# A block-diagonal product in two matmuls of 288 columns, and its result copied out of PSUM by ScalarE before the norm

## The chip, the cores and the metric

The kernel runs on one core of a Trainium2 chip. The metric is the device time of one execution in microseconds; the kernel before has a median of 944.4 us in 3 runs (943.82 to 945.24). The profile shown is of one execution of 944.21 us, whose instructions span 942.4 us, at a mean granted TensorE clock of 0.999.

A core has engines that run beside each other: TensorE (in the profile PE for its matmuls and PEld for its weight loads), VectorE (DVE), ScalarE (ACT), GpSimd (POOL) and SyncE (SP), which here issues the transfers. TensorE writes its results to PSUM, a memory of eight banks of 512 fp32 columns over 128 partitions; VectorE and ScalarE read them there and write to the large memory, SBUF.

## The reference

A linear attention with a norm, whose result is the input of a gated pair of matrix products:

```python
# q, k, v: (8, 8, 576, 64), g_norm: (64,)
kv  = einsum('bhsd,bhse->bhde', k, v)            # 64 x 64 for each head
out = einsum('bhsd,bhde->bhse', q, kv)
rms = sqrt(mean(out * out, axis=-1, keepdims=True) + 1e-6)
x   = out / rms * g_norm                         # then (B, H, S, D) -> (B*S, H*D) = 4608 x 512
# w_in: (512, 2048), w_out: (2048, 512), float64
h  = x @ w_in
sp = max(h, 0) + log1p(exp(-abs(h)))             # softplus
y  = (h * erf(sp)) @ w_out                       # 4608 x 512
```

## The kernel before

Two heads are handled at once, as the two diagonal 64x64 blocks of a 128x128 matrix. There are 8 batch entries (T = 0 to 7) with 4 pairs of heads each (p = 0 to 3): 32 attention steps. Of the 576 rows of a pair, 512 are the main part (G = 512) and 64 the tail (R = 64); the tails of all entries are gathered in `x_last` and go through norm and products as a ninth group (T = 8). The attention steps of group T+1 are dealt out as small pieces between the large products of group T, whose matmuls are at line 462 (`n_ps`, `m_ps`) and, for the first two groups, at lines 520 and 692.

The pieces of one step, with the lines of the profile at the side. `halves` is true for T = 2 to 7, so for 24 of the 32 steps. `bank(...)` gives one of two PSUM tiles of one bank each (`ps_at`).

```python
def products():
    kv_ps = st["kv"] = bank("kv_ps")
    for c in range(C):                           # L297: k^T v, both heads
        for i in range(2):
            nc.tensor.matmul(kv_ps[s, s], lhsT=ks[rows, i, c], rhs=vs[rows, i, c], ...)
    if p % 2 == 0:                               # L305: the tails of two pairs, transposed
        nc.tensor.transpose(kv_ps[:, q_tail], q_last[:, p // 2], ident)
    ...
    for i in range(2):                           # L312: the blocks into bd
        nc.vector.tensor_copy(out=bd[s, s], in_=kv_ps[s, s])
    if p % 2 == 0:                               # L315
        nc.vector.tensor_copy(out=tails[T], in_=kv_ps[:, q_tail])
    st["tail"] = tails[T][:, p % 2 * R : p % 2 * R + R]
    qt_ps = bank("qt_ps")
    for j in range(J):                           # L319: q transposed
        nc.tensor.transpose(qt_ps[:, j * P : j * P + P], qs[:, j], ident)
    nc.scalar.copy(st["qT"], qt_ps)              # L320

def apply():
    qT, o_ps, kv_ps = st["qT"], bank("se_ps"), st.pop("kv")
    nc.tensor.matmul(kv_ps[:, o_tail], lhsT=bd, rhs=st.pop("tail"), ...)   # L324: 64 columns
    nc.tensor.matmul(o_ps, lhsT=bd, rhs=qT, ...)                           # L325: 512 columns
    nc.vector.tensor_copy(out=x_last[:, p, T * R : T * R + R], in_=kv_ps[:, o_tail])
    st["o"] = o_ps
    nc.scalar.activation(qT, o_ps, AF.Square)    # L328

def halve():                                     # the squares as a sum of two fp32r tiles
    nc.vector.tensor_copy(out=hi, in_=sq)        # L338
    nc.vector.tensor_tensor(out=lo, in0=sq, in1=hi.bitcast(FP32), op=ALU.subtract)

def mean(table=True):
    ms = st["ms"] = bank("ms_ps")
    if halves:                                   # L346, L347
        nc.tensor.matmul(ms, lhsT=mean_w, rhs=st.pop("hi"), start=True, stop=False)
        nc.tensor.matmul(ms, lhsT=mean_w, rhs=st.pop("lo"), start=False, stop=True)
    ...
    nc.scalar.activation(r, ms, AF.Ln, bias=eps_col)      # L358
    nc.scalar.activation(r, r, AF.Exp, scale=-0.5)        # L359
    nc.scalar.activation(u, r, AF.Square)                 # L360

def norm():                                      # L366, L369, L378
    nc.vector.scalar_tensor_tensor(out=u, in0=ms, scalar=EPS, in1=u, ...)
    nc.vector.scalar_tensor_tensor(out=u, in0=u, scalar=3.0, in1=r, ...)
    nc.vector.scalar_tensor_tensor(out=x, in0=st.pop("o"), scalar=gm_col, in1=u, ...)

def split():                                     # L405, L408, L411
    thirds(st.pop("x"), *(form[:, p] for form in x_forms[T]))
```

`x_forms` are the three fp32r forms of the normed `x` (a high part, a low part and a scaled sum) that the products at line 462 take. Each of those products is eight matmuls into `n_ps` (high and low part) and four into `m_ps` (the sum), each of 512 columns.

Of the kernel before, what the change touches and what calls it, by code (L numbers as in the profile page):

```python
# [39 lines left out]
FP32 = mybir.dt.float32  # L40
# [3 lines left out]
AF = mybir.ActivationFunctionType  # L44
ALU = mybir.AluOpType
PSUM = bass.MemoryType.PSUM
# [8 lines left out]
FIRST = 2  # L55
# [5 lines left out]
def kernel(  # L61
# [10 lines left out]
    nc = tc.nc  # L72
    P = 128
    B, H, S, D = q.shape
    DM, DF = moe_w_in.shape[0], moe_w_in.shape[1] // 2
    J = 4
    G = J * P
    R = S - G
# [8 lines left out]
    attp = ctx.enter_context(tc.tile_pool(name="attp", bufs=1))  # L87
# [5 lines left out]
    first_w = room.enter_context(tc.tile_pool(name="first_w", bufs=1, side="right"))  # L93
    gate = room.enter_context(tc.tile_pool(name="gate", bufs=7, side="right"))
    early = early_room.enter_context(tc.tile_pool(name="early", bufs=2))
    ps_at = ctx.enter_context(tc.tile_pool(name="ps_at", bufs=2, space=PSUM))
    ps_h = ctx.enter_context(tc.tile_pool(name="ps_h", bufs=2, space=PSUM))
    ps_o = ctx.enter_context(tc.tile_pool(name="ps_o", bufs=1, space=PSUM))

    ctx.enter_context(tc.manual_schedule())  # L100

# [51 lines left out]
    for i in range(2):  # L153
        nc.gpsimd.dma_start(
            out=g_col[i * D : i * D + D, :], in_=g_norm.rearrange("(d one) -> d one", one=1)
# [11 lines left out]
    ident = const.tile([P, P], FP32, name="ident")  # L167
    make_identity(nc, ident)
    mean_w = const.tile([P, P], FP32R, name="mean_w")
# [13 lines left out]
    x_last = const.tile([P, KC, G], FP32, name="x_last")  # L183
# [79 lines left out]
    xT, x_forms, tails = {}, {}, {}  # L263
# [5 lines left out]
    def attention(T, p, pools=None):  # L269

        st = {}

        halves = FIRST <= T < B
        bd = bd_kv[:, (T * NP + p) % 2, :]

        q_tail, o_tail = slice(P, 2 * P), slice(2 * P, 2 * P + R)

        def bank(name):
            pool, tag = (pools or {}).get(name, (ps_at, "at"))
            return pool.tile([P, G], FP32, name=name, tag=tag)  # L280

        def square_tile(name):

            if T == 0:
                return gate.tile([P, G], FP32, name=name, tag="h")
            return attp.tile([P, G], FP32, name=name, tag="qT")

        def products():

            kv_ps = st["kv"] = bank("kv_ps")  # L290
            ks, vs, qs = (x.pop((T, p)) for x in (k_sb, v_sb, q_sb))
            C = chunks(T)
            for c in range(C):
                rows = slice(0, S // C + (c < S % C))
                for i in range(2):
                    s = slice(i * D, i * D + D)
                    nc.tensor.matmul(  # L297
                        kv_ps[s, s],
                        lhsT=ks[rows, i, c],
                        rhs=vs[rows, i, c],  # L300
                        start=(c == 0),
                        stop=(c == C - 1),
                    )
            if p % 2 == 0:
                nc.tensor.transpose(kv_ps[:, q_tail], q_last[:, p // 2], ident)  # L305
            if p == NP - 2:
                for i in range(NP):
                    load_last(T + 1, i)
            st["qT"] = square_tile("qT")
            for i in range(2):  # L310
                s = slice(i * D, i * D + D)
                nc.vector.tensor_copy(out=bd[s, s], in_=kv_ps[s, s])  # L312
            if p % 2 == 0:
                tails[T] = attp.tile([P, P], FP32, name="qT_last", tag="t")
                nc.vector.tensor_copy(out=tails[T], in_=kv_ps[:, q_tail])  # L315
            st["tail"] = tails[T][:, p % 2 * R : p % 2 * R + R]
            qt_ps = bank("qt_ps")
            for j in range(J):
                nc.tensor.transpose(qt_ps[:, j * P : j * P + P], qs[:, j], ident)  # L319
            nc.scalar.copy(st["qT"], qt_ps)  # L320

        def apply():
            qT, o_ps, kv_ps = st["qT"], bank("se_ps"), st.pop("kv")
            nc.tensor.matmul(kv_ps[:, o_tail], lhsT=bd, rhs=st.pop("tail"), start=True, stop=True)  # L324
            nc.tensor.matmul(o_ps, lhsT=bd, rhs=qT, start=True, stop=True)  # L325
# [4 lines that stand above are left out]
        def square():  # L330
            st["o"], st["qT"] = x_last[:, p, :], square_tile("sq")
            nc.scalar.activation(st["qT"], st["o"], AF.Square)

        def halve():
            sq = st.pop("qT")
            hi = st["hi"] = attp.tile([P, G], FP32R, name="sq_hi", tag="rms_r")
            lo = st["lo"] = attp.tile([P, G], FP32R, name="sq_lo", tag="sq_lo")
            nc.vector.tensor_copy(out=hi, in_=sq)  # L338
            nc.vector.tensor_tensor(out=lo, in0=sq, in1=hi.bitcast(FP32), op=ALU.subtract)

        def mean(table=True):
            ms = st["ms"] = bank("ms_ps")
            if halves:


                nc.tensor.matmul(ms, lhsT=mean_w, rhs=st.pop("hi"), start=True, stop=False)  # L346
                nc.tensor.matmul(ms, lhsT=mean_w, rhs=st.pop("lo"), start=False, stop=True)  # L347
                u = square_tile("u")
            else:
                u = st.pop("qT")  # L350
                nc.tensor.matmul(ms, lhsT=mean_w.bitcast(FP32), rhs=u, start=True, stop=True)  # L351
            if T > 0:
                r = attp.tile([P, G], FP32, name="rms_r", tag="rms_r")
                exp_ln_table()
            else:
                r = gate.tile([P, G], FP32, name="rms_r", tag="s")
            st["u"], st["r"] = u, r
            nc.scalar.activation(r, ms, AF.Ln, bias=eps_col)  # L358
            nc.scalar.activation(r, r, AF.Exp, scale=-0.5)  # L359
            nc.scalar.activation(u, r, AF.Square)  # L360
            if table and (T > 0 or p == NP - 1):
                softplus_table()

        def norm():
            ms, u, r = (st.pop(name) for name in ("ms", "u", "r"))
            nc.vector.scalar_tensor_tensor(  # L366
                out=u, in0=ms, scalar=EPS, in1=u, op0=ALU.add, op1=ALU.mult
            )
            nc.vector.scalar_tensor_tensor(  # L369
                out=u, in0=u, scalar=3.0, in1=r, op0=ALU.subtract, op1=ALU.mult  # L370
            )
            if T < FIRST:
                if T not in xT:
                    xT[T] = wide.tile([P, KC, G], FP32, name="xT", tag="ab"[T])
                x = xT[T][:, p, :]
            else:
                x = st["x"] = x_new.tile([P, G], FP32, name="x", tag="x")
            nc.vector.scalar_tensor_tensor(  # L378
                out=x,
                in0=st.pop("o"),  # L380
                scalar=gm_col,
                in1=u,
                op0=ALU.mult,
                op1=ALU.mult,
            )

        def split():
            if T >= FIRST:
                thirds(st.pop("x"), *(form[:, p] for form in x_forms[T]))

        def loads():
            load_pair(T * NP + p + 2)

        if T == 0:
            return products, apply, halve, mean, norm
        if T == B:
            return lambda: None, square, lambda: None, mean, norm, split

        pieces = ((products,), (apply,), (halve, loads)) if halves else ((products, loads), (apply,), ())
        return (*(partial(chain, *group) for group in pieces), mean, norm, split)  # L400


# [111 lines left out]
    o_ps = {}  # L514
# [129 lines left out]
    for n in range(FIRST * FC + 1):  # L644
        T, f = divmod(n, FC)
        if n == FC:
            early_room.close()
            late = ctx.enter_context(tc.tile_pool(name="late", bufs=1))
            x_new = ctx.enter_context(tc.tile_pool(name="x_new", bufs=1))
            acc = ctx.enter_context(tc.tile_pool(name="acc", bufs=1))  # L650
            w_in_p = ctx.enter_context(tc.tile_pool(name="w_in_p", bufs=BATCH))
            low = low_room.enter_context(tc.tile_pool(name="low", bufs=1))
            forms = late.tile([P, 3, KC, G], FP32R, name="x_forms0")
            x_forms[FIRST] = [forms[:, i] for i in range(3)]
# [25 lines left out]
        elif T < FIRST:  # L680
# [10 lines left out]
            for i, c in blocks:  # L691
                nc.tensor.matmul(  # L692
                    plain[i],
                    lhsT=w_in_sb[:, c, i % FC * P : i % FC * P + P],
                    rhs=xT[T][:, c, :],
                    start=(c == 0),
                    stop=(c == KC - 1),
# [89 lines left out]
    for m in range(first_batch, batches + 1):  # L787
        T, b = divmod(m, NB)
# [127 lines left out]
```

## Time and profile before

| | |
|---|---|
| median of 3 runs | 944.4 us (943.82 to 945.24) |
| span of the profiled execution | 942.4 us |
| product and result of one attention step among the large products, from 500.94 to 525.67 us | 24.73 us |
| in it: TensorE, VectorE, ScalarE busy | 24.73, 19.94, 15.91 us |
| the copy of `qt_ps` (L320), the square of `se_ps` (L328) | 584, 580 ns |
| Ln, Exp, Square of the mean (L358, L359, L360) | 688, 632, 633 ns |
| norm (L366, L369, L378) | 684, 691, 751 ns |
| one table load on ScalarE | 1283 ns |

The profile names a group of instructions by its line, its engine and what it writes and reads (out<-in). A mean duration of a matmul's record is not its cost: the records overlap, and their ends are modelled. What one costs is the distance between its start and that of the next.

The timeline gives start and duration of each run of equal instructions, in us from the span's start; what stands in brackets is the idle time of the engine before it, and what ended it.

### The profile page before, as it was taken

The numbers are of one execution on the slowest core, as the hardware profiler recorded it, in microseconds if no ns is written. First come the engines' busy times: TensorE is split into PE (matmuls) and PEld (weight loads), VectorE is DVE, ScalarE is ACT, GpSimd is POOL, SyncE is SP. The second block draws the span as 40 slices with busy tenths as digits, with TensorE's granted clock in tenths as the row PEclk, the third lists the DMA queues.
The fourth block names the chain that finished last, engine by engine and source line by source line (L and its number), as shares of the span: only waits on it lengthen the run. The fifth ranks groups of instructions, "written<-read, shape, count | busy, mean of one in ns | idle before, by whom it ended". The sixth has DMA issues, their size and how long they took to land.

```text
span 942.4 us, 11743 instructions
## 1 busy us (share of the span) xinstructions
PE 924.8 (98%) x4272; PEld 683.4 (73%) x4272; DVE 742.6 (79%) x1056; ACT 615.6 (65%) x825; POOL 2.4 (0%) x10
## 2 busy tenths in 40 slices
PE   6999999999999999999999999999999999999997
PEld 4444445666688888888888888888888888888886
DVE  3999858887577787877778888878887877787667
ACT  3899776776766666666666666666666666665551
POOL 1000000000000000000000000000000000000000
PEclk9999999999999999999999999999999999999999
DMA  9766406899699998998899889998896778778871
GB/s 257 276 204 207 150 1 227 318 351 335 214 363 335 309 325 283 306 311 307 280 287 314 294 298 309 311 303 296 293 325 260 263 253 345 284 286 287 353 263 46
DMA packets 111842, 259.78 MB, mean 276 GB/s; under 512 B 43864, under 2 KB 69544, under 8 KB 111784
## 3 DMA queue, kind: packets, MB, share of 16 engines
q1 hardware_dynamic: 110152, 256.73, 78.7%
q10 hardware_dynamic: 1568, 2.29, 0.8%
q8 instruction: 34, 0.56, 0.2%
q14 instruction: 24, 0.20, 0.1%
q0 software_dynamic: 64, 0.00, 0.0%
HBM read 224.40 MB, written 34.60 MB: 275 GB/s over the span
## 4 chain that ended last, share of the span: by engine, by line
PE 92%; DVE 4%; DMA 2%; ACT 1%; issue 0%; SPq 0%; DVEq 0%
PE n_ps L462 45%; PE m_ps L462 22%; PE o_ps L520 10%; PE h_ps L692 6%; PE se_ps L325 3%; PE kv_ps L297 2%; PE qt_ps L319 2%; DMA w_raw<-in_moe_w_in_dram 1%; PE ms_ps L351 1%; DMA v_sb<-in_v_dram 1%; DVE h L876 1%; DVE e L445 1%; PE ms_ps L346 1%; PE ms_ps L347 1%; PE kv_ps L324 1%; DVE e L440 0%
## 5 line engine op out<-in xcount | busy, mean ns | idle before, releaser
L462 PE MATMUL n_ps<-x_forms,w_in_parts 128*128 128x512 f32 x896 | 232.5, 401 | 0.1
L462 PE MATMUL n_ps<-w_out_parts,g_forms 128*128 128x512 f32 x928 | 231.2, 391 | 0.0
L462 PEld LDWEIGHTS n_ps<-w_out_parts,g_forms 128*128 128x128 f32 x928 | 174.2, 188 | 38.4 <-issue 1.4
L462 PEld LDWEIGHTS n_ps<-x_forms,w_in_parts 128*128 128x128 f32 x896 | 166.8, 188 | 43.1 <-issue 9.3
L852 ACT ACTIVATE s<-h 128x512 f32<-128x512 f32 x112 | 71.0, 633 | 178.9 <-DVE h L445 178.9
L445 DVE TENSOR_TENSOR h<-m_ps,h 128x512 f32<-128x512 f32 x116 | 79.7, 687 | 59.8 <-ACT h L837 43.8
L462 PE MATMUL m_ps<-w_out_parts,g_forms 128*128 128x512 f32 x464 | 124.2, 389 | 0.0
L462 PE MATMUL m_ps<-x_forms,w_in_parts 128*128 128x512 f32 x448 | 120.0, 390 | 0.0
L520 PE MATMUL o_ps<-w_out_sb,h_sb 128*128 128x512 f32 x224 | 100.8, 593 | 0.3 <-DVE h_sb L642 0.3
L462 PEld LDWEIGHTS m_ps<-w_out_parts,g_forms 128*128 128x128 f32 x464 | 87.1, 188 | 18.0
L462 PEld LDWEIGHTS m_ps<-x_forms,w_in_parts 128*128 128x128 f32 x448 | 84.1, 188 | 17.7
L445 DVE TENSOR_TENSOR e<-m_ps,e 128x512 f32<-128x512 f32 x116 | 80.2, 692 | 18.2 <-PE m_ps L462 10.9
L440 DVE SCALAR_TENSOR_TENSOR e<-n_ps,e 128x512 f32<-128x512 f32 x88 | 60.3, 685 | 39.2 <-PE n_ps L462 39.2
L520 PEld LDWEIGHTS o_ps<-w_out_sb,h_sb 128*128 128x128 f32 x224 | 42.3, 190 | 48.9 <-issue 46.6
L411 DVE SCALAR_TENSOR_TENSOR g_forms<-g_forms 128x1024 fp32r<-128x1024 f32 x58 | 71.1, 1225 | 2.0
L408 DVE TENSOR_TENSOR g_forms<-h,g_forms 128x1024 fp32r<-128x1024 f32 x58 | 70.6, 1217 | 1.7 <-ACT g_forms L405 1.4
L876 DVE TENSOR_TENSOR h<-h,s 128x1024 f32<-128x1024 f32 x58 | 68.3, 1218 | 0.7 <-ACT s L856 0.7
L837 ACT ACTIVATE h<-n_ps 128x512 f32<-128x512 f32 x112 | 65.5, 585 | 3.4 <-PE n_ps L462 3.4
L405 ACT ACTIVATE g_forms<-h 128x1024 fp32r<-128x1024 f32 x58 | 58.9, 1059 | 12.2 <-PE m_ps L462 8.7
L692 PE MATMUL h_ps<-xT,w_in_sb 128*128 128x512 f32 x144 | 64.9, 594 | 0.7 <-DVE w_in_sb L240 0.6
L106 ACT ACT_TABLE_LOAD x44 | 56.5, 1283 | 0.8
L856 ACT ACTIVATE s<-s 128x1024 f32<-128x1024 f32 x56 | 56.2, 1052 | 0.3
(98 smaller groups left out, 1013.3 us busy)
## 6 DMA issues: line engine op xcount, KB each, us to landing
w_out_parts<-w_out SPq DMA_DIRECT2D x116, 768.0 KB
w_in_parts<-w_in SPq DMA_DIRECT2D x112, 768.0 KB
w_in<-w_new SPq DMA_DIRECT2D x16, 768.0 KB
q_sb<-in_q_dram SPq DMA_DIRECT2D x32, 256.0 KB
w_raw<-in_moe_w_out_dram SPq DMA_DIRECT2D x8, 1024.0 KB
out_dram<-e SPq DMA_DIRECT2D x32, 256.0 KB
k_sb<-in_k_dram SPq DMA_DIRECT2D x28, 287.5 KB
v_sb<-in_v_dram SPq DMA_DIRECT2D x28, 287.5 KB
```

The lines of the kernel that those rows point to most:

```text
L106: nc.scalar.preload_act_table_set("softplus")
L405: nc.scalar.activation(high, x, AF.Copy, scale=1.0 + 2.0**-13)
L408: nc.vector.tensor_tensor(out=low, in0=x, in1=high.bitcast(FP32), op=ALU.subtract)
L411: nc.vector.scalar_tensor_tensor(out=both, in0=low.bitcast(FP32), scalar=SHIFT, in1=high.bitcast(FP32), op0=ALU.mult, op1=ALU.add,)
L440: nc.vector.scalar_tensor_tensor(out=out_, in0=ps, scalar=scale, in1=out_, op0=ALU.mult, op1=ALU.add)
L445: nc.vector.tensor_tensor(out=out_, in0=ps, in1=out_, op=ALU.add)
L462: nc.tensor.matmul(ps, lhsT=weights(form, k), rhs=moving(form, k), start=(form == forms[0] and k == 0), stop=(form == forms[-1] and k == 3),)
L520: nc.tensor.matmul(o_ps[j], lhsT=g[:, j * P : j * P + P], rhs=w_out_sb[:, f, :], start=(f == 0), stop=last,)
L692: nc.tensor.matmul(plain[i], lhsT=w_in_sb[:, c, i % FC * P : i % FC * P + P], rhs=xT[T][:, c, :], start=(c == 0), stop=(c == KC - 1),)
L837: nc.scalar.activation(h[:, i], n_ps, AF.Copy, scale=SHIFT - 1.0)
L852: nc.scalar.activation(s[:, i], h[:, i], AF.Softplus)
L876: nc.vector.tensor_tensor(out=part(h, half), in0=part(h, half), in1=part(s, half), op=ALU.mult)
```

## The change

For the 24 steps with `halves`, one PSUM tile of two banks takes the place of the two tiles of one bank. Each bank holds one half of the work: first kv and the tail in one and the transposed q in the other, then, in each, 256 columns of the main result and 32 of the tail, and at last 256 columns of the mean beside the result. So the product with the block-diagonal matrix is two matmuls of 288 columns, where it was one of 512 and one of 64, and the mean is two times two matmuls of 256 columns. The transposed q and the tail are therefore laid side by side in SBUF, in two rows of 288. To give the one tile back early, ScalarE copies the result (into `x`) and the mean (into `ms_sb`) to SBUF, and the norm reads them there. The other steps keep the two tiles of one bank, whose pool is closed when the second group begins.

The diff, cut to its core:

```diff
         def bank(name):
+            if T >= FIRST:
+                return two_banks()[:, name in ("qt_ps", "se_ps")]
             pool, tag = (pools or {}).get(name, (ps_at, "at"))
             return pool.tile([P, G], FP32, name=name, tag=tag)
+        def two_banks():
+            if "two" not in st:
+                st["two"] = ps_two.tile([P, 2, G], FP32, name="at_ps", tag="at")
+            return st["two"]
+        HG, HR = G // 2, R // 2
...
         def products():
...
+            if halves:
+                tail = tails.pop(T) if p % 2 else kv_ps[:, P : P + R]
+                nc.vector.tensor_copy(out=st["qT"][:, :, HG:], in_=twofold(tail))
+                if p % 2 == 0:
+                    tails[T] = attp.tile([P, R], FP32, name="qT_next", tag="t")
+                    nc.vector.tensor_copy(out=tails[T], in_=kv_ps[:, P + R : 2 * P])
...
+            if halves:
+                nc.scalar.copy(st["qT"][:, :, :HG], twofold(qt_ps))
...
         def apply():
+            if halves:
+                qT, two = st.pop("qT"), two_banks()
+                for i in range(2):
+                    nc.tensor.matmul(
+                        two[:, i, : HG + HR], lhsT=bd, rhs=qT[:, i], start=True, stop=True
+                    )
+                nc.vector.tensor_copy(
+                    out=twofold(x_last[:, p, T * R : T * R + R]), in_=two[:, :, HG : HG + HR]
+                )
+                o_ps = two[:, :, :HG]
+                qT = st["qT"] = qT[:, :, :HG]
+                nc.scalar.activation(qT, o_ps, AF.Square)
+                x = st["x"] = x_new.tile([P, G], FP32, name="x", tag="x")
+                st["o"] = twofold(x)
+                nc.scalar.copy(st["o"], o_ps)
+                return
...
         def mean(table=True):
-            ms = st["ms"] = bank("ms_ps")
+            ms = st["ms"] = two_banks()[:, :, HG:] if halves else bank("ms_ps")
             if halves:
-                nc.tensor.matmul(ms, lhsT=mean_w, rhs=st.pop("hi"), start=True, stop=False)
-                nc.tensor.matmul(ms, lhsT=mean_w, rhs=st.pop("lo"), start=False, stop=True)
+                hi, lo = (twofold(st.pop(name)) for name in ("hi", "lo"))
+                for i in range(2):
+                    nc.tensor.matmul(ms[:, i], lhsT=mean_w, rhs=hi[:, i], start=True, stop=False)
+                    nc.tensor.matmul(ms[:, i], lhsT=mean_w, rhs=lo[:, i], start=False, stop=True)
...
             nc.scalar.activation(r, ms, AF.Ln, bias=eps_col)
+            if halves:
+                st["ms"] = twofold(attp.tile([P, G], FP32, name="ms_sb", tag="sq_lo"))
+                nc.scalar.copy(st["ms"], ms)
             nc.scalar.activation(r, r, AF.Exp, scale=-0.5)
...
         if n == FC:
             early_room.close()
+            at_room.close()
+            ps_two = ctx.enter_context(tc.tile_pool(name="ps_two", bufs=1, space=PSUM))
```

More of the change, by code (lines that the diff above doesn't have):

```diff
@@ L95 @@
     early = early_room.enter_context(tc.tile_pool(name="early", bufs=2))
-    ps_at = ctx.enter_context(tc.tile_pool(name="ps_at", bufs=2, space=PSUM))
     ps_h = ctx.enter_context(tc.tile_pool(name="ps_h", bufs=2, space=PSUM))
     ps_o = ctx.enter_context(tc.tile_pool(name="ps_o", bufs=1, space=PSUM))
+    at_room = ctx.enter_context(ExitStack())
+    ps_at = at_room.enter_context(tc.tile_pool(name="ps_at", bufs=2, space=PSUM))
     ctx.enter_context(tc.manual_schedule())
@@ L278, in bank, with twofold, square_tile @@
         def bank(name):
+            if T >= FIRST:
+                return two_banks()[:, name in ("qt_ps", "se_ps")]
             pool, tag = (pools or {}).get(name, (ps_at, "at"))
             return pool.tile([P, G], FP32, name=name, tag=tag)
-        def square_tile(name):
+        def two_banks():
[3 more added lines that the diff above has]
+        HG, HR = G // 2, R // 2
+        def twofold(x):
+            return x.rearrange("p (i n) -> p i n", i=2) if halves else x
+        def square_tile(name, tail=False):
             if T == 0:
                 return gate.tile([P, G], FP32, name=name, tag="h")
-            return attp.tile([P, G], FP32, name=name, tag="qT")
+            t = attp.tile([P, 2, HG + HR], FP32, name=name, tag="qT")
+            if tail:
+                return t
+            return t[:, :, :HG] if halves else t.rearrange("p i n -> p (i n)")[:, :G]
         def products():
@@ L305, in products @@
                 nc.tensor.transpose(kv_ps[:, q_tail], q_last[:, p // 2], ident)
+            qt_ps = bank("qt_ps")
+            for j in range(J):
+                nc.tensor.transpose(qt_ps[:, j * P : j * P + P], qs[:, j], ident)
             if p == NP - 2:
@@ L308, in products @@
                     load_last(T + 1, i)
-            st["qT"] = square_tile("qT")
+            st["qT"] = square_tile("qT", halves)
             for i in range(2):
@@ L312, in products @@
                 nc.vector.tensor_copy(out=bd[s, s], in_=kv_ps[s, s])
[L313 to L320, printed above, removed]
-        def apply():
+            if halves:
[4 more added lines that the diff above has]
+                    nc.vector.tensor_copy(out=tails[T], in_=kv_ps[:, P + R : 2 * P])
+            else:
+                if p % 2 == 0:
+                    tails[T] = early.tile([P, P], FP32, name="qT_last", tag="t", bufs=1)
+                    nc.vector.tensor_copy(out=tails[T], in_=kv_ps[:, q_tail])
+                st["tail"] = tails[T][:, p % 2 * R : p % 2 * R + R]
+            if halves:
+                nc.scalar.copy(st["qT"][:, :, :HG], twofold(qt_ps))
+            else:
+                nc.scalar.copy(st["qT"], qt_ps)
+        def apply():
+            if halves:
+                qT, two = st.pop("qT"), two_banks()
+                del st["kv"]
+                for i in range(2):
[12 more added lines that the diff above has]
+                return
             qT, o_ps, kv_ps = st["qT"], bank("se_ps"), st.pop("kv")
@@ L337, in halve @@
             lo = st["lo"] = attp.tile([P, G], FP32R, name="sq_lo", tag="sq_lo")
-            nc.vector.tensor_copy(out=hi, in_=sq)
-            nc.vector.tensor_tensor(out=lo, in0=sq, in1=hi.bitcast(FP32), op=ALU.subtract)
+            nc.vector.tensor_copy(out=twofold(hi), in_=sq)
+            nc.vector.tensor_tensor(
+                out=twofold(lo), in0=sq, in1=twofold(hi.bitcast(FP32)), op=ALU.subtract
+            )
         def mean(table=True):
-            ms = st["ms"] = bank("ms_ps")
+            ms = st["ms"] = two_banks()[:, :, HG:] if halves else bank("ms_ps")
             if halves:
-                nc.tensor.matmul(ms, lhsT=mean_w, rhs=st.pop("hi"), start=True, stop=False)
-                nc.tensor.matmul(ms, lhsT=mean_w, rhs=st.pop("lo"), start=False, stop=True)
+                hi, lo = (twofold(st.pop(name)) for name in ("hi", "lo"))
+                for i in range(2):
+                    nc.tensor.matmul(ms[:, i], lhsT=mean_w, rhs=hi[:, i], start=True, stop=False)
+                    nc.tensor.matmul(ms[:, i], lhsT=mean_w, rhs=lo[:, i], start=False, stop=True)
                 u = square_tile("u")
@@ L352, in mean @@
             if T > 0:
-                r = attp.tile([P, G], FP32, name="rms_r", tag="rms_r")
+                r = twofold(attp.tile([P, G], FP32, name="rms_r", tag="rms_r"))
                 exp_ln_table()
@@ L375, in norm @@
                 x = xT[T][:, p, :]
+            elif halves:
+                x = st["x"]
             else:
@@ L378, in norm @@
             nc.vector.scalar_tensor_tensor(
-                out=x,
+                out=twofold(x),
                 in0=st.pop("o"),
```

## The prediction

> **What bounds the kernel now.** I read the page first: the engines' shares, and the busy digits over 40 slices.
>
> ```profile
> PE 924.8 (98%) x4272; PEld 683.4 (73%) x4272; DVE 742.6 (79%) x1056; ACT 615.6 (65%) x825; POOL 2.4 (0%) x10
> PE   6999999999999999999999999999999999999997
> DVE  3999858887577787877778888878887877787667
> ACT  3899776776766666666666666666666666665551
> ```
>
> TensorE is busy in every slice but the first and the last, at a granted clock of 0.999. A busy TensorE can still hide waits, because the ends of its matmuls are modelled. So next came the list of waits, for TensorE and for its weight loads (PEld). Columns: who waited, for whom, total us, times, longest us.
>
> ```profile
> PE kv_ps L297 <- DMA v_sb<-in_v_dram: 8.9, 4, 6.5
> PE ms_ps L351 <- ACT rms_r L358: 1.3, 1, 1.3
> PEld kv_ps L297 <- DVE x L378: 6.7, 19, 0.4
> ```
>
> The first two belong to the first 35 us. The third is the only one that recurs, and it is the wait the change could remove: the first weight load of each attention step stands idle until the previous step's last norm instruction (L378, the reader of `se_ps`) gives its bank back. Is it real? The timeline in order of time around one such place, and around one in an earlier stage where no norm was pending:
>
> ```profile
> 523.53 1.07 PE L462 MATMUL m_ps<-w_out_parts,g_forms 128*128 128x512 f32 x4
> 524.53 0.80 PE L297 MATMUL kv_ps<-v_sb,k_sb 116*64 116x64 f32 x20
> ...
> 141.79 0.59 PE L520 MATMUL o_ps<-w_out_sb,h_sb 128*128 128x512 f32 x1
> 142.31 0.80 PE L297 MATMUL kv_ps<-v_sb,k_sb 116*64 116x64 f32 x20
> ```
>
> Late: four matmuls at 0.227 make 0.91, and kv starts 1.00 after the first of them, so 0.09 is lost. Early: one at 0.43, and kv starts 0.52 later, again 0.09 lost. The same gap without a pending norm says that the 0.09 belongs to the switch from full-width to 116x64 weights. I count nothing for removing the wait.
>
> So what counts is TensorE's own time. The steps with split squares (`halves`, T from 2 to 7) are 24: L346 stands 24 times. Their product, in the same timeline:
>
> ```profile
> 503.79 1.98 PE L462 MATMUL n_ps<-x_forms,w_in_parts 128*128 128x512 f32 x8
> 505.61 1.08 PE L462 MATMUL m_ps<-x_forms,w_in_parts 128*128 128x512 f32 x4
> 506.52 0.33 PE L324 MATMUL kv_ps<-qT_last,bd_kv 128*128 128x64 f32 x2
> 507.20 2.40 PE L462 MATMUL n_ps<-x_forms,w_in_parts 128*128 128x512 f32 x8
> 509.44 1.07 PE L462 MATMUL m_ps<-x_forms,w_in_parts 128*128 128x512 f32 x4
> ```
>
> Eight matmuls of 512 columns in fp32r take 505.61 - 503.79 = 1.82 (0.227 each). From the start of the 64-column product to the next m_ps it is 509.44 - 506.52 = 2.92, so the two products together cost 2.92 - 1.82 = 1.10 us. And the mean:
>
> ```profile
> 515.79 0.39 PE L346 MATMUL ms_ps<-sq_hi,mean_w 128*128 128x512 f32 x1
> 516.03 0.39 PE L347 MATMUL ms_ps<-sq_lo,mean_w 128*128 128x512 f32 x1
> 516.26 2.00 PE L462 MATMUL n_ps<-w_out_parts,g_forms 128*128 128x512 f32 x8
> ```
>
> It costs 516.26 - 515.79 = 0.47 us.
>
> **What the Trainium skill says.** "TensorE: Matmul & The Clock Gate", section "LDWEIGHTS (loading the stationary operand)", gives a load as its columns over 1.2 per ns: 107 ns for 128 columns. The trace agrees where it can show it: the 64-column product stands as two records, as every fp32 matmul does here, each with its own load, and their share of the 1.10 comes out below as 0.12 each, twice what streaming 64 columns should need. The same page, "Back-to-back issue gap", makes the gap proportional to the columns plus some 2.5 ns; fp32 records of 512 columns stand 0.43 apart here (two passes), fp32r ones 0.227, about 12 ns more than half of that.
>
> "ScalarE: Activation LUTs", section "What ACT_TABLE_LOAD costs", gives 186 ns + 0.833 ns a column for an activation without pointer operands, 612 ns for 512; the trace has 584 for the copy of `qt_ps`, and I use that.
>
> "PSUM — Partial Sum Buffer", "Summary: rules for kernel authors", asks that a bank be read while a matmul fills a different one. With kv and q transposed in one tile of two banks, the next step's kv product has to wait for every reader of this one. The trace of before can't show that wait, since its tile is new.
>
> **The change, part by part.**
>
> *Block-diagonal product.* Removed: one of 64 columns and one of 512. Added: two of 288. The columns are the same 576, the weight loads too (four records). Two records of 512 cost 2 x 0.43 = 0.86, so the 64-column pair took 1.10 - 0.86 = 0.24, although at 0.43 per 512 columns it should stream in 2 x 0.054 = 0.11. It is bound by its weight loads. A record of 288 columns takes 0.43 x 288/512 = 0.242, well over a load; four make 0.97. Saved: 0.13, from rounded starts; I take 0.12 a step, times 24 = 2.9 us, all on TensorE's path.
>
> *Mean.* Two fp32r matmuls of 512 columns become four of 256. An estimate: half of 0.215 to stream, plus the 12 ns: 0.12 each, 0.48 against 0.47. The load, some 0.11, lies just under that. Cost 0.01 to 0.02 a step, 0.4 us in all.
>
> *kv and q transposes.* TensorE's order is unchanged: kv, tail, four transposes. Only the bank bookkeeping differs.
>
> *ScalarE.* Two copies more a step, 2 x 0.585 = 1.17 us, 28 us in all. In a step of 24.7 us ScalarE is busy 15.9, so it becomes 17.1. Both lie in front of the norm:
>
> ```profile
> 519.74 0.69 ACT L358 ACTIVATE rms_r<-ms_ps,eps_col 128x512 f32<-128x512 f32 x1
> 520.47 0.64 ACT L359 ACTIVATE rms_r<-rms_r 128x512 f32<-128x512 f32 x1
> 521.13 0.63 ACT L360 ACTIVATE u<-rms_r 128x512 f32<-128x512 f32 x1
> 522.08 0.68 DVE L366 SCALAR_TENSOR_TENSOR u<-ms_ps,u 128x512 f32<-128x512 f32 x1
> ```
>
> The copy of the result delays the evacuations after it, and so the last softplus, erf and Ln, by 0.59; the copy of the mean delays `u` by as much again. `u` then comes at 521.76 + 1.17 = 522.93 and the norm about 0.85 later. TensorE needs none of this: with the copies the banks are free after the mean's copy, near 521.6, and kv starts at 524.5, some 2.9 us later. Before, L378 ended at 524.27, just in time.
>
> *VectorE.* The norm's last instruction reads SBUF instead of PSUM, perhaps 0.06 less (0.75 against 0.69 for L369, which reads SBUF alone); the tail goes in two small copies of some 0.2 on even steps instead of one of 0.29. About even, and VectorE has 4.8 us free in a step of 24.7.
>
> Sum: 2.9 saved, 0.4 lost: 944.4 - 2.5 = 941.9. I round toward nothing changed, for small waits at the borders named below: **942.1 us**.
>
> **Rivals.**
>
> *The mean is bound by its weight loads.* A weight load's record lasts 0.188, and if four matmuls of 256 columns in fp32r could not follow one another faster than 0.227, the mean would cost 0.91 instead of 0.47: 24 x 0.44 = 10.6 us lost, 952 us. Against it: the 64-column fp32 pair, whose loads have records as long, goes at 0.12 a record. For it: no fp32r matmul of fewer than 512 columns stands in this trace.
>
> *The later norm stops TensorE where T changes.* There the step's last quarter of `x_forms` is needed at once: in the step at 351 us VectorE ends the low part at 352.74 and the sum at 353.47; n_ps started at 352.26 and comes to its eighth matmul at about 353.9, m_ps to its fourth at about 354.9. The slack is 1.1 to 1.4, the norm 0.85 later. If I am short by half a microsecond, six such borders cost 3 us: about 945.
>
> *The wait for the bank was real.* Then up to 0.09 in 20 steps, 1.8 us more: about 940.3. The equal gap of the early stage speaks against it.
>
> *Two banks held by one tile, without a second buffer, make kv wait.* The ScalarE copies would have to slip by 2.9 us. If they did by a microsecond more, 24 us: 966. ScalarE's 7 us of idle time a step speak against it.
>
> **Range and chances.** Everything sure is within 3 us of 944.4; the first two rivals lie above. 8 in 10: 940.5 to 945.2. A change of 2% is 18.9 us: faster has no mechanism at all, slower only through the last rival. Faster 0.01, within 2% 0.97, slower 0.02.
>
> **What would show it.** From the start of the 288-column product to the m_ps after the next eight matmuls: 2.79 instead of 2.92. Starts of the four mean matmuls about 0.12 apart; 0.227 would be the first rival. From the last m_ps before kv to kv still 0.32, with or without a wait on the list. ScalarE some 28 us busier, `u` about 1 us later in the step, VectorE waiting for it, and the step of 24.78 shorter by 0.1. The prediction is wrong if the mean's matmuls don't halve, or if n_ps or kv start waiting for the norm or for a ScalarE copy.

## The result, and the profile after

The changed kernel takes 990.0 us (989.5 to 990.5 in 4 runs) where the kernel before took 944.2 beside it: a ratio of 1.0484, with a 95% interval of 1.0466 to 1.0502. 45.9 us were lost; I had said 942.1, with 945.2 as the upper end. The lines of the two programs differ: L462 is now L519, L297 is L316, L325 (and L324) is L357, L346 and L347 are L398 and L399, L320 is L348, L378 is L435. VectorE's copy of the blocks out of kv (L312) is L335, and L338 and L341 are its copies of the tails. The last Square for `u` and the norm's first instruction (L360, L366) are L415 and L421, the high part of the squares (L338) is L386, and the first two of the three forms (L405, L408) are L462 and L465.

The page of the changed kernel, engines' shares first, then the chain that ended last, by engine:

```profile
PE 937.5 (95%) x4320; PEld 687.8 (70%) x4320; DVE 746.7 (76%) x1080; ACT 636.6 (64%) x873; POOL 2.4 (0%) x10
PE 41%; DVE 25%; ACT 25%; issue 6%; DMA 2%; SPq 0%; DVEq 0%; ACTq 0%
```

The same line of the chain in the kernel before:

```profile
PE 92%; DVE 4%; DMA 2%; ACT 1%; issue 0%; SPq 0%; DVEq 0%
```

No engine has become the bound by its work: VectorE and ScalarE are busy for a smaller share of the span than before. But half of the chain now runs through these two in equal parts. They wait for each other. The list of waits of the changed kernel says where (who waited, for whom, total us, times, longest us):

```profile
DVE u L421 <- ACT u L415: 45.3, 22, 3.8
ACT qT L348 <- DVE qT_next L341: 43.6, 12, 4.3
ACT qT L348 <- DVE bd_kv L335: 41.0, 11, 3.9
DVE g_forms L465 <- ACT g_forms L462: 31.7, 21, 1.7
PE at_ps L398 <- DVE sq_hi L386: 16.5, 19, 1.1
```

ScalarE stands for 84.6 us in front of its copy of the transposed q, for VectorE. Before, in the same 24 steps, it stood there for 22.4 us, and for TensorE alone. Then VectorE waits for ScalarE twice in a step, and TensorE for VectorE at the mean (and for 5.3 us in all for the copy of q itself, ahead of the product). One such place in the timeline of the changed kernel, engines in turn:

```profile
574.82 0.60 PE L328 MATMUL at_ps<-ident,q_sb 128*128 128x128 f32 x4
...
575.07 0.75 DVE L435 SCALAR_TENSOR_TENSOR x<-x,gm_col,u 128x512 f32<-128x512 f32 x1
...
579.85 0.45 DVE L335 COPY bd_kv<-at_ps 64x64 f32<-64x64 f32 x2
...
580.46 0.22 DVE L341 COPY qT_next<-at_ps 128x64 f32<-128x64 f32 x1
580.76 0.59 ACT L348 COPY qT<-at_ps 128x512 f32<-128x512 f32 x1 [4.27 <-DVE qT_next L341]
581.24 2.00 ACT L462 ACTIVATE g_forms<-h 128x1024 fp32r<-128x1024 f32 x2
582.34 1.23 DVE L465 TENSOR_TENSOR g_forms<-h,g_forms 128x1024 fp32r<-128x1024 f32 x1 [1.66 <-ACT g_forms L462]
```

The four transposes of q start at 574.82, 0.11 apart, and ScalarE has been free since 576.5. It copies them at 580.76, right after VectorE's last read of kv. VectorE got to kv so late because the rest of the norm, four sums and two forms of x stand ahead of it in its order. Behind ScalarE's copy stand the two activations for `g_forms`, and for the first of them VectorE waits in turn. The same place before, from the kernel before:

```profile
501.23 0.59 ACT L320 COPY qT<-qt_ps 128x512 f32<-128x512 f32 x1 [1.13 <-PE qt_ps L319]
501.71 2.01 ACT L405 ACTIVATE g_forms<-h 128x1024 fp32r<-128x1024 f32 x2
503.46 0.45 DVE L312 COPY bd_kv<-kv_ps 64x64 f32<-64x64 f32 x2
504.13 1.21 DVE L408 TENSOR_TENSOR g_forms<-h,g_forms 128x1024 fp32r<-128x1024 f32 x1
```

There ScalarE copied q 2.2 us before VectorE touched kv, and `g_forms` was ready when VectorE came for it.

The reason for the wait can be read from which instruction is named. On even steps it is L341, on odd ones L335: each time VectorE's last read of the two-bank tile `at_ps`. On odd steps L338 comes after it and writes a part of the very tile qT that ScalarE writes too, and that isn't waited for; in an odd step of the changed kernel ScalarE starts while L338 still runs:

```profile
607.55 0.20 DVE L338 COPY qT<-qT_next 128x64 f32<-128x64 f32 x1
...
607.60 0.58 ACT L348 COPY qT<-at_ps 128x512 f32<-128x512 f32 x1 [3.90 <-DVE bd_kv L335]
```

So the order is kept for the PSUM tile, although the two engines read different banks of it. Two engines do read two banks at once elsewhere: in the kernel before, VectorE's sum over `m_ps` runs from 519.20 to 519.89, and ScalarE's Ln reads `ms_ps` from 519.74 on. The wait comes with the shared tile.

### The profile page after: what moved, and what is told of

The parts are those of the page before. It is cut to its first block, busy times and chain, and to the rows that moved or that the text cites. A ratio compares the mean times of both kernels' runs of the same rounds, so it can differ in the third digit from the quotient of the medians.

```text
span 987.7 us, 12034 instructions
## 1 busy us (share of the span) xinstructions
PE 937.5 (95%) x4320; PEld 687.8 (70%) x4320; DVE 746.7 (76%) x1080; ACT 636.6 (64%) x873; POOL 2.4 (0%) x10
## 4 chain that ended last, share of the span: by engine, by line
PE 41%; DVE 25%; ACT 25%; issue 6%; DMA 2%; SPq 0%; DVEq 0%; ACTq 0%
PE n_ps L519 16%; PE o_ps L577 8%; PE m_ps L519 8%; PE h_ps L751 6%; DVE h L502 5%; DVE g_forms L465 4%; ACT s L915 4%; DVE e L502 3%; ACT L105 3%; ACT s L911 3%; ACT L915 2%; ACT h L896 2%; DVE e L497 2%; ACT g_forms L462 2%; DVE x L435 2%
## 5 line engine op out<-in xcount | busy, mean ns | idle before, releaser
L519 PE MATMUL n_ps<-x_forms,w_in_parts 128*128 128x512 f32 x896 | 230.3, 398 | 5.3 <-DVE x_forms L465 4.1
L519 PE MATMUL n_ps<-w_out_parts,g_forms 128*128 128x512 f32 x928 | 231.4, 391 | 0.0
L519 PEld LDWEIGHTS n_ps<-w_out_parts,g_forms 128*128 128x128 f32 x928 | 172.8, 188 | 36.8 <-issue 1.7
L519 PEld LDWEIGHTS n_ps<-x_forms,w_in_parts 128*128 128x128 f32 x896 | 166.8, 188 | 42.8 <-DVE x_forms L465 6.0
L519 PE MATMUL m_ps<-w_out_parts,g_forms 128*128 128x512 f32 x464 | 124.0, 389 | 0.0
L519 PE MATMUL m_ps<-x_forms,w_in_parts 128*128 128x512 f32 x448 | 120.0, 390 | 0.0
L519 PEld LDWEIGHTS m_ps<-w_out_parts,g_forms 128*128 128x128 f32 x464 | 87.1, 188 | 18.1
L519 PEld LDWEIGHTS m_ps<-x_forms,w_in_parts 128*128 128x128 f32 x448 | 84.1, 188 | 17.6
L465 DVE TENSOR_TENSOR g_forms<-h,g_forms 128x1024 fp32r<-128x1024 f32 x58 | 70.7, 1219 | 31.7 <-ACT g_forms L462 31.7
L348 ACT COPY qT<-at_ps 128x512 f32<-128x512 f32 x24 | 14.1, 585 | 84.5 <-DVE qT_next L341 43.6
L462 ACT ACTIVATE g_forms<-h 128x1024 fp32r<-128x1024 f32 x58 | 58.8, 1056 | 12.2 <-PE m_ps L519 8.7
```

Source lines behind the costliest of these rows:

```text
L462: nc.scalar.activation(high, x, AF.Copy, scale=1.0 + 2.0**-13)
L465: nc.vector.tensor_tensor(out=low, in0=x, in1=high.bitcast(FP32), op=ALU.subtract)
L519: nc.tensor.matmul(ps, lhsT=weights(form, k), rhs=moving(form, k), start=(form == forms[0] and k == 0), stop=(form == forms[-1] and k == 3),)
```

## The experiments

Theory W is this wait. Rival C, from the prediction's own sums, is the two added ScalarE copies, whose delay I had called harmless. Rival B is the single tile without a second buffer.

The table gathers all runs. The step is the mean distance between starts of kv over the last fifteen distances, in the timeline of each. "Shared tile" is the one of two banks.

| kernel | us | against before | step, us |
|---|---|---|---|
| before | 944.2 to 944.6 | | 24.78 |
| changed | 990.0 | +45.9 | 27.09 |
| shared tile, q copied first, both copies | 959.7 | +15.4 | 25.46 |
| shared tile, old order, no copies | 974.4 | +30.1 | 26.30 |
| shared tile, q copied first, no copies | 943.9 | -0.7 | 24.72 |
| shared tile, q copied first, both copies, square and copy moved | 945.7 | +1.2 | 24.72 |
| before with the wait | 985.9 | +41.6 | 26.54 |
| before with one copy | 947.2 | +2.7 | 24.85 |
| before with two copies | 956.6 | +12.3 | 25.38 |
| before with three copies | 970.8 | +26.3 | 26.01 |
| shared tile, q copied first, no copies, square first too | 944.6 | +0.1 | 24.72 |
| shared tile, q copied first except for T = 2, no copies | 943.4 | -1.0 | 24.72 |

**The copy of q issued first.** Only the program's order is changed:

```diff
             st["qT"] = square_tile("qT", halves)
+            if halves:
+                nc.scalar.copy(st["qT"][:, :, :HG], twofold(qt_ps))
             for i in range(2):
                 nc.vector.tensor_copy(out=bd[s, s], in_=kv_ps[s, s])
...
-            if halves:
-                nc.scalar.copy(st["qT"][:, :, :HG], twofold(qt_ps))
-            else:
+            if not halves:
                 nc.scalar.copy(st["qT"], qt_ps)
```

> The changed kernel, with ScalarE's copy of the transposed q issued ahead of VectorE's reads of kv instead of after them. Theory W (in program order the copy stands behind VectorE's reads of the same two-bank PSUM tile, and ScalarE, which works in order, is blocked there): 940 to 947 us, idle time of ScalarE before that copy down from 84.5 us to about 35 us. Rival C (the two added ScalarE copies make every later piece of the step late): 980 us or more. Rival B (one tile without a second buffer): 980 us or more.

Measured: 959.7 us, a ratio of 1.016 (1.0143 to 1.0177). 30.3 of the 45.9 us are gone, but W alone had promised all of them: both theories missed. ScalarE's wait for VectorE at that copy is gone; what remains is this wait of VectorE for `u`:

```profile
DVE u L421 <- ACT u L415: 40.9, 21, 3.8
```

**The changed kernel without the two copies.** The norm reads PSUM again:

```diff
-                x = st["x"] = x_new.tile([P, G], FP32, name="x", tag="x")
-                st["o"] = twofold(x)
-                nc.scalar.copy(st["o"], o_ps)
+                st["o"] = o_ps
...
-            if halves:
-                st["ms"] = twofold(attp.tile([P, G], FP32, name="ms_sb", tag="sq_lo"))
-                nc.scalar.copy(st["ms"], ms)
```

> The changed kernel without the two added ScalarE copies: the norm reads the result and the mean in PSUM, as before the change. Theory W: ScalarE still blocks at the copy of the transposed q, and the next step's kv must now also wait for the norm on VectorE: 985 to 1015 us. Rival C: 942 to 950 us.

Measured: 974.4 us (1.0316; 1.0295 to 1.0337), below what W had said and far above C. The wait at the copy of q is untouched (43.5 and 41.0 us). With it the norm is late and kv now waits for it, as W had it: in one place m_ps starts at 564.13 and kv at 566.63, 2.50 where 1.00 is usual. Without the copies the loss is smaller all the same. Added up, the 15.4 with the copies alone and the 30.1 with the wait alone give 45.5, and the change lost 45.9: two causes, nearly independent.

**The kernel before, with the two copies only.**

```diff
             nc.scalar.activation(qT, o_ps, AF.Square)
+            if halves:
+                x = st["x"] = st["o"] = x_new.tile([P, G], FP32, name="x", tag="x")
+                nc.scalar.copy(x, o_ps)
...
             nc.scalar.activation(r, ms, AF.Ln, bias=eps_col)
+            if halves:
+                st["ms"] = attp.tile([P, G], FP32, name="ms_sb", tag="sq_lo")
+                nc.scalar.copy(st["ms"], ms)
```

> The kernel before, with only the two ScalarE copies added (result and mean to SBUF, the norm reads them there), in the old two tiles of one bank and with the old products of 512 and 64 columns. Theory W: 943 to 950 us, ScalarE 28 us busier. Rival C: 980 us or more.

Measured: 956.6 us (1.0128; 1.0108 to 1.0148). That lies above W's range and far below C's. So the copies cost 12.3 us without any shared tile.

**The kernel before, with the wait only.**

```diff
+            if halves:
+                nc.scalar.copy(seen[D:, :], bd[D:, P - 1 :] if p % 2 else tails[T][D:, P - 1 :])
             nc.scalar.copy(st["qT"], qt_ps)
```

> The kernel before, with only the wait added: ahead of its copy of the transposed q ScalarE copies one column of what VectorE has just copied out of the kv bank (the diagonal blocks on odd steps, the tail on even ones), so it can't pass before VectorE has got there. Theory W: 975 to 995 us, with ScalarE idle some 80 us at that place. Rivals B and C: 944 to 952 us.

Measured: 985.9 us (1.0438; 1.0417 to 1.0459), as W had it. The added copies of one column take 0.19 us each, 4.6 us in all; what they wait for is in the list:

```profile
ACT seen L322 <- DVE bd_kv L313: 40.4, 11, 3.8
ACT seen L322 <- DVE qT_last L316: 40.1, 11, 4.2
```

80.5 us, nearly the changed kernel's 84.6. That it costs 41.6 here and 30.1 there may lie in these added copies, or in the old two tiles, where TensorE's transposes then stand 10.5 us for the norm's bank; that was not tried apart.

What the copies do became a second theory, R. The step is a ring: from the last softplus through erf, Ln and Exp to `u` on ScalarE; from the norm through the sums and forms to the next `h` on VectorE; and back to softplus. TensorE's 24.8 us set the pace only while the ring is shorter. In the kernel before, `u` ends at 521.76 and VectorE begins the norm at 522.08, when its last sums are done: a slack of some 0.3 at that place. Work that goes into the ring beyond its slack should come back in every step.

**One copy, and three.** For one, only the copy of the mean was added to the kernel before; for three, the kernel with both copies makes that of the mean twice:

```diff
             if halves:
                 st["ms"] = attp.tile([P, G], FP32, name="ms_sb", tag="sq_lo")
                 nc.scalar.copy(st["ms"], ms)
+                nc.scalar.copy(st["ms"], ms)
```

> The kernel before with one ScalarE copy added, that of the mean. With both copies it took 956.6, 12.3 more. Theory R: 0.58 us is just about the slack of the ring, so little comes through: 944 to 947 us. Rival L (linear in ScalarE's time): 950.5 us.

> The kernel before with the copies of the result and of the mean, the latter made twice. Theory R: the third copy of 0.58 us comes through whole in nearly every step, 12 to 15 us on top of 956.6: 967 to 973 us. Rival L: 962.8 us.

Measured: 947.2 us (1.0028; 1.0019 to 1.0037) with one, just above R's range, and 970.8 (1.0273; 1.0252 to 1.0293) with three, within it; L is out both times. The copies cost 2.7, then 9.6, then 14 us: a slack, and then nearly the full price.

The steps give the sizes. A copy lasts 0.58 us, but that is not what it adds to the ring. From the start of Ln to the end of `u` it is 2.02 us in the kernel before (519.74 to 521.76), and with the mean copied once 2.36, as here in the changed kernel:

```profile
571.22 0.69 ACT L410 ACTIVATE rms_r<-at_ps,eps_col 128x512 f32<-128x512 f32 x1
571.81 0.58 ACT L413 COPY ms_sb<-at_ps 128x512 f32<-128x512 f32 x1
...
572.95 0.63 ACT L415 ACTIVATE u<-rms_r 128x512 f32<-128x512 f32 x1
```

With the mean copied twice it is 2.98. From the square of the result to ScalarE's next activation it is 0.48, and 0.94 with the copy of the result between them. So the copy of the mean adds 0.34, that of the result 0.46, the second one of the mean 0.62. With two copies the step is 25.38; less 0.80, that puts the ring of the kernel before at 24.58, only 0.2 under TensorE's 24.78 (an estimate). It fits the other two runs: with three copies 26.00, where 26.01 was measured, and with one 24.92, where the last six distances have a mean of 24.93. VectorE's waits for `u`, in the kernel before and with one, two and three copies:

```profile
DVE u L366 <- ACT u L360: 4.2, 2, 3.4
```

```profile
DVE u L369 <- ACT u L363: 18.4, 19, 3.8
```

```profile
DVE u L372 <- ACT u L366: 41.2, 21, 3.8
```

```profile
DVE u L373 <- ACT u L367: 57.8, 24, 4.4
```

The delay also needs time to reach TensorE. With two copies the first four steps after 252 us are still 24.7 to 24.9 each; the fifth, at the border between two groups, takes 25.66, and from there on about one step in four is free of it.

**Both causes removed.** The transposed q first, and the norm from PSUM: the first two edits together.

> The changed kernel with ScalarE's copy of the transposed q ahead of VectorE's reads, and without the two added copies (the norm reads PSUM, so kv waits for the norm as before the change). Theory R (the step is a ring: ScalarE's chain from the last softplus to u, then VectorE from the norm to the next sums, then ScalarE again; the copies of the result and the mean lie in it, and what they add beyond a slack of some 0.5 us a step comes back in every step): with the copies gone the ring is as short as before, and only TensorE's saving is left: 940 to 944.5 us. Rival H (holding both banks in one tile until the norm is done costs more than the copies): 955 us or more.

Measured: 943.9 us (0.9991; 0.9984 to 0.9997). The steps, which were 24.72 and 24.84 by turns, are 24.65 and 24.77: 0.07 less, TensorE's saving, at last. Holding the one tile until the norm is done costs nothing in these steps. Rival B is out, and H with it.

**The same work, placed elsewhere.** From the run with q first, with both copies: the square and the copy of the result go where ScalarE waits for VectorE's sum anyway, and VectorE's copy of the tail after them. In the diff, `pieces(i + 1)` deals out the step's next pieces, these among them; the change of order within `apply()` is left out.

```diff
                 evacuate()
+                if i == 1:
+                    pieces(i + 1)
                 nc.scalar.activation(s[:, i], h[:, i], AF.Softplus)
             pieces(i + 1)
```

> The changed kernel with the copy of the transposed q first, and with the square and the copy of the result moved ahead of the second softplus, where ScalarE stands idle 1.9 us a step, and VectorE's copy of the tail after them. The same work on every engine as in the run with the transposed q first (959.7). Theory R: the square leaves the ring and the copy of the mean takes its place in it: 940 to 945 us. Rival L (ScalarE's added busy time costs by itself, wherever it stands): 955 us or more.

Measured: 945.7 us (1.0008; 1.0000 to 1.0017), just above R's range, against 959.7 with the same instructions. The step is 24.72 too, and VectorE's waits for `u` are down from 40.9 us:

```profile
DVE u L421 <- ACT u L415: 4.9, 2, 3.8
```

So it was the place of the copies in the ring and not ScalarE's added work: ScalarE is busy for 636.4 us here and for 635.6 in the run with 959.7, where the kernel before had 615.6. What keeps it above 944 lies before 256 us: that stage, where the steps of T = 2 stand among the second group's products, takes 112.1 us from kv to kv over four steps, against 109.6 before.

**The rest in that stage.** Without the copies, too, it lost 0.8 us (110.4). Two guesses. First, that ScalarE's square waits for VectorE's copy of the tail there (3.2 us), in the shared tile again:

```diff
-                nc.vector.tensor_copy(out=twofold(x_last[...]), in_=two[:, :, HG : HG + HR])
                 o_ps = two[:, :, :HG]
                 nc.scalar.activation(qT, o_ps, AF.Square)
+                nc.vector.tensor_copy(out=twofold(x_last[...]), in_=two[:, :, HG : HG + HR])
```

> The run with the transposed q first and the norm in PSUM (943.9), with ScalarE's square of the result also ahead of VectorE's copy of the tail, which reads the same two banks. Theory W (in a shared tile whoever reads second in program order waits): ScalarE's 3.2 us of waiting for that copy in the second group's stage (142 to 256 us) and TensorE's waits for the mean there, about 1 us, go: 942.4 to 943.6 us, some 1.5 us under the kernel before, which is what TensorE's 0.07 us a step in 24 steps can give. Otherwise: 943.9 as it was.

Measured: 944.6 us (1.0003; 0.9995 to 1.0012). That is above W's range: the 3.2 us of waiting went and nothing was won; the stage took 111.0. Second, that the new order itself is the wrong one there: with q first, this stage has a wait the other way round, from VectorE's list of the run with both causes removed, between 142 and 256 us:

```profile
DVE bd_kv L337 <- ACT qT L334: 6.8, 4, 2.5
```

So the old order was put back for these four steps:

```diff
-            if halves:
+            if halves and T > FIRST:
                 nc.scalar.copy(st["qT"][:, :, :HG], twofold(qt_ps))
...
+            if halves and T == FIRST:
+                nc.scalar.copy(st["qT"][:, :, :HG], twofold(qt_ps))
```

> The run with the transposed q first and the norm in PSUM (943.9), but with the old order, VectorE's reads of kv ahead of ScalarE's copy of the transposed q, in the four steps of T = 2, which lie in the second group's stage (142 to 256 us). Theory W: there ScalarE is the one behind, and with the copy first VectorE waited for it, 6.8 us in four steps; with the old order that goes, and the 0.8 us that this stage lost against the kernel before comes back: 942.8 to 943.5 us. Otherwise (something else in that stage): 943.9 or more.

Measured: 943.4 us (0.9989; 0.9981 to 0.9998), and the stage takes 109.6. It is the best version found, 1.0 us under the kernel before (0.2 to 1.8 by the interval).

## Why the prediction was wrong

**"Only the bank bookkeeping differs."** This sentence on the kv and q transposes is the step that failed most, with 30 of the 46 us. In its place stood a wait of 84.6 us: ScalarE's copy of q behind VectorE's reads of kv. I asked only what TensorE waits for when it fills the shared tile, and not who waits for whom when it is read. The Trainium skill, "PSUM — Partial Sum Buffer", section "Terms", says that two engines on one bank and quadrant at once collide, reads against reads included, so some order is needed within a bank. Here it was kept between two banks of one tile as well, and no run shows a collision. My fourth rival was close: it had one tile as the trouble, but with kv waiting for it. Kv waits for ScalarE in the list only: it starts 0.32 after the last m_ps, as I had said.

**"The norm about 0.85 later. TensorE needs none of this."** The second failure, with 15 us (12.3 on the kernel before). That the copies delay `u` was right, and for one step 0.85 was even too much: they add 0.80, not 1.17, less the slack. But I compared a delay with TensorE's reserves of 1.1 to 2.9 us once, as if the next step began afresh. The delay isn't caught up in "7 us of idle time a step"; those idle times are waits for the other engine. It adds 0.6 a step until the reserves are gone. With two copies on the kernel before, the norm's last instruction starts 1.3 us after kv (555.33 against 554.02), where it started 1.0 before it (523.52 against 524.53). At five borders n_ps then waits for `x_forms`, 3.8 us in all in TensorE's list, where the kernel before has none: the sign that I had named. My second rival (the borders between the groups) had the place where it breaks through first, and its "six such borders cost 3 us" is the same mistake.

**TensorE's sums.** They held, a little high. From the 288-column product to the m_ps after eight more matmuls it is 2.82 us (581.86 to 584.68 in the step above), where I had 2.79 and the kernel before 2.92. The mean's matmuls do halve. From the run with both causes removed, where none of them waits:

```profile
590.04 0.28 PE L396 MATMUL at_ps<-sq_hi,mean_w 128*128 128x256 f32 x1
590.16 0.28 PE L397 MATMUL at_ps<-sq_lo,mean_w 128*128 128x256 f32 x1
...
590.52 2.00 PE L512 MATMUL n_ps<-w_out_parts,g_forms 128*128 128x512 f32 x8
```

The four take 0.48, 0.12 each, as I had said, so my first rival is out. Together the step saves 0.07 where I had 0.10. In the best version, the last nineteen distances between starts of kv are together 1.1 us shorter than before (469.73 against 470.87), and the four steps of T = 2 save nothing (109.6 in both). That makes its 1.0 us instead of 2.5; why those four save nothing stays open.

**The wait of kv for the norm** in the kernel before was indeed no loss: with it or without it the gap is the same 0.09.

**VectorE** was to gain 0.06 by reading SBUF in the norm's last instruction. It gained nothing: 752 ns, against 751 from PSUM.

## What to carry to other kernels

When two tiles become one, list every reader of the new tile in program order: here one engine was blocked behind another, though they read different banks, and whatever stood behind the blocked instruction waited too. Issue first the read whose engine gets there first, which may differ from stage to stage. An engine's idle time is no slack if it is spent waiting for an engine that waits for it: measure the ring against the bound, count what an added instruction delays rather than how long it lasts, and put added work outside the ring.

## What the runs showed of the hardware that was not expected

Records of fp32 matmuls of 288 columns take just their share: in the second group's stage of the changed kernel four of them take 0.97 us (203.03 to 204.00), and 0.97 was worked out from 0.43 for 512 columns. And ScalarE copies two runs of 256 columns out of two banks as fast as 512 in one: 578 ns for the result and the mean, 585 for the transposed q, against 584 before.
